# Attention and maxout network in one kernel: batch 2's row sums through one bank, broadcasts of batches 2 to 4 in the queue of the loads, and attention work in fewer, larger visits

## The chip, the cores and the metric

The kernel runs on one core of a Trainium2 chip. Its engines work side by side, each on its own list of instructions in order: TensorE (PE; its weight loads are shown apart as PEld), VectorE (DVE), ScalarE (ACT), GpSimd (POOL) and SyncE (SP). DMA engines move data, and DMAs are issued by POOL (in the profile's queue q0) and by SP (queue q1). Matrix products go to eight banks of PSUM memory, which DVE and ACT empty. The metric is the device time of one execution in microseconds (us): 407.24 us before the change, the median of three runs between 407.20 and 407.46.

## The reference, cut to what matters

There are 8 batches of 8 heads with 1024 positions of 64 numbers. Keys and values are first projected from 1024 positions down to 64, then every query attends to these 64, and the result goes through a network that takes the maximum of three products.

```python
k_proj = np.einsum('ks,bhsd->bhkd', E, k)
v_proj = np.einsum('ks,bhsd->bhkd', F, v)
scores = scale * np.matmul(q, k_proj.transpose(0, 1, 3, 2))
scores = scores - np.max(scores, axis=-1, keepdims=True)
attn = np.exp(scores)
attn = attn / (np.sum(attn, axis=-1, keepdims=True) + 1e-09)
attn_out = np.matmul(attn, v_proj)
x = attn_out.transpose(0, 2, 1, 3).reshape(B * S, H * D)      # 8192 x 512
h = np.maximum(np.maximum(x @ w1, x @ w2), x @ w3)            # 8192 x 768
out = h @ w_out                                               # 8192 x 512
```

## The kernel before, in words

The order of every engine is written out by hand. Batches follow one another, and each batch b is two chunks (`ch` 0 and 1) of 512 rows of the network. A chunk has six up steps (`up`, one for each 128 columns of h: 12 matmuls at L567, then a copy on ACT at L625 and two maxima on DVE at L629 and L577), and four down steps (`down`: six matmuls at L664, a copy of the result to `o_sb`, and after every second one an output store from SP). So PE's list is this network work, and between the steps stand visits of attention work for the *next* batch n = b + 1. The function `plan(b)` says which. Its key (ch, step) is the place: steps 0 to 5 are the up steps, 6 to 9 the down steps, and the work listed stands behind that step.

The pieces of attention work are these. `ld(b)` has POOL issue the loads of q, k and v of a batch (L200), each 1 MB as it lands; the tiles of k and v exist once, so k and v of a batch can only be issued after the projections of the batch before, and q only after the transposition of the q before it. `qd` copies q into another order on DVE and has SP issue a DMA transposition (L392). `kproj` and `vproj` project k and v (L345, 16 small matmuls each), `kt` turns the projected keys. A batch has four pairs of heads. `sc(n, g)` is one pair's score product (L211, four matmuls of 64x64 that run side by side, into two banks), followed by an exponential on ACT (L222) that frees these banks. With `now` the exponential is put into ACT's list at once; without it, behind the next `o_sb` copy or `h1s` copy (`run_later`). `za` takes a pair's row sums (four matmuls with ones, L231), their reciprocals on ACT (logarithm L291 and exponential L297), the value product (L231) and the multiplication on DVE (L308). `zc` and `vx` do the same work in another way: `zc` takes the sums of all four pairs into one bank (L256), their reciprocals (L262, L265), writes these 32 KB to the scratch tile `zd` in device memory (L268), and spreads them to all partitions with four broadcast DMAs of 512 KB into `zi_all` (L275), all issued by SP; `vx` is then the value product and the multiplication alone.

Banks are dealt when the program is built: `bank()` and `two()` take what a rough clock of the planner says comes free first. The real wait is a semaphore: a matmul that writes a bank waits for whoever read it last.

Before the change, batch 1 and batch 2 use `za`; batches 3 to 7 use `zc` and `vx`. Batch 2's four pairs are spread over five visits in batch 1's turn, batch 3's scores over two visits of two pairs, batch 4's scores stand one in batch 2's turn and three in batch 3's, and later batches' scores stand together in one visit with a value product between them.

Of the kernel before, what the change touches and what calls it, by code (L numbers as in the profile page):

```python
# [15 lines left out]
def kernel(  # L16
# [13 lines left out]
    nc = tc.nc  # L30
# [12 lines left out]
    NPAIR = H // 2  # L43
# [93 lines left out]
    def load_tiles(b):  # L137
        qkv[b] = tuple(
            loads.tile([P, H, SI, D], BF16, name=nm, bufs=n)
            for nm, n in (("q_t", 2), ("k_t", 1), ("v_t", 1))  # L140
        )
        return qkv[b]
# [51 lines left out]
    load_w(2, slice(2, 4))  # L194
    nc.gpsimd.dma_start(out=wout_sb, in_=moe_w_out.rearrange("(jt p) m -> p jt m", p=P))

    def load(b):
        tiles = load_tiles(b)
        for i in range(3):
            dma = nc.gpsimd.dma_start(out=tiles[i], in_=view((q, k, v)[i], b))  # L200
            if i == 0 and b - 1 in last_T:
                after(dma, last_T[b - 1])
# [42 lines left out]
            zi_alls[b] = att.tile([P, NPAIR, 2, CHUNK], FP32, name="zi_all", bufs=1)  # L245
        return zi_alls[b]

    def zc(b):

        def f():
            t, ns = bank()
            for hp in range(2):
                for g in range(NPAIR):
                    nc.tensor.matmul(  # L256
                        out=t[32 * g:32 * (g + 1), :], lhsT=pick[:, hp, :],
                        rhs=pTs[b, g, 0][:, hp, :], start=(hp == 0), stop=(hp == 1),
                    )
            ready = pe(2 * MM + 0.1)  # L260
            zlc = att.tile([P, CHUNK], FP32, name="zlc", bufs=1)
            nc.scalar.activation(out=zlc, in_=t, func=AF.Ln)  # L262
            runs("s", ready, 0.6, ns)
            zic = att.tile([P, CHUNK], FP32, name="zic", bufs=1)
            nc.scalar.activation(out=zic, in_=zlc, func=AF.Exp, scale=-1.0)  # L265
            when = runs("s", ready, 0.63) + 9.0
            zd = scratch.tile([NPAIR, 2, 2, CHUNK], FP32, name="zd")
            nc.sync.dma_start(  # L268
                out=zd.rearrange("g h c f -> (g h c) f"),
                in_=zic.rearrange("(a r) f -> a r f", r=8)[:, 0, :],  # L270
            )
            for u in range(2):
                gs = slice(2 * u, 2 * u + 2)
                for hp in range(2):
                    nc.sync.dma_start(  # L275
                        out=zi_all(b)[hp * HALF:(hp + 1) * HALF, gs],
                        in_=zd[gs, hp].partition_broadcast(HALF),
                    )
            for g in range(NPAIR):
                zis[b, g, 0] = zi_all(b)[:, g], when  # L280
        return f
# [98 lines left out]
    def qd(b, parts=1):  # L380

        def f():
            q_p = att.tile([P, NPAIR, SI, 2, D], BF16, name="q_p", bufs=1)
            qTs[b] = att.tile([P, NPAIR * SI, P], BF16, name="qT")
            n = NPAIR // parts
            for lo in range(0, NPAIR, n):
                for g in range(lo, lo + n):
                    copy(
                        "v", q_p[:, g].rearrange("p si h d -> p h si d"),
                        qkv[b][0][:, 2 * g:2 * g + 2], (), 0.43,  # L390
                    )
                last_T[b] = nc.sync.dma_start_transpose(  # L392
                    out=qTs[b][:, lo * SI:(lo + n) * SI, :],
                    in_=q_p[:, lo:lo + n].rearrange("p g si h d -> p (g si h d)"),
                )
        return f

    kps = {}
    def kproj(b):
        def f():  # L400
            t, ns = bank()
            proj(b, 1, t, (LO, HI), 4 * D)
            kps[b] = att.tile([P, 2, 2 * D], BF16, name="kp")
            copy("v", kps[b].rearrange("a g x -> a (g x)"), t[:, 0:4 * D], ns, 0.43)
        return f
# [18 lines left out]
    def vproj(b):  # L424
        def f():
            t, ns = bank()
            proj(b, 2, t, (LO, HI), 4 * D)

            vps[b] = att.tile([P, H, D], BF16, name="vp")
            for hh, hs in enumerate((LO, HI)):  # L430
                i = t[hh * HALF:(hh + 1) * HALF, 0:4 * D].rearrange("a (h d) -> a h d", d=D)
                for to in range(2):
                    copy("sv"[hh], vps[b][to * HALF:(to + 1) * HALF, hs, :], i, ns, 0.4)
        return f
# [244 lines left out]

    def ld(b):
        return lambda: load(b)

    def plan(b):
        n = b + 1
        if b == 0:
            c1 = (SPC, SPC)
            return {
                (0, 6): [za(0, 1, *c1), sc(0, 3, *c1)],  # L690
                (0, 7): [qd(1, 2), za(0, 2, *c1)],
                (0, 8): [za(0, 3, *c1)],
                (1, 0): [kproj(1)],
                (1, 1): [kt(1)],
                (1, 2): [vproj(1), ld(2)],
                (1, (3, "mid")): [sc(1, 0), sc(1, 1)],
                (1, 4): [za(1, 0), sc(1, 2)],
                (1, 5): [za(1, 1), sc(1, 3)],
                (1, 7): [za(1, 2), za(1, 3)],
            }  # L700
        if b == 1:
            return {
                (0, 1): [qd(2)],
                (0, 5): [kproj(2), vproj(2), ld(3)],
                (0, 6): [kt(2)],
                (0, 7): [sc(2, 0)],
                (0, 9): [za(2, 0), sc(2, 1)],
                (1, 1): [za(2, 1), sc(2, 2)],
                (1, 3): [za(2, 2), sc(2, 3)],
                (1, 5): [za(2, 3)],  # L710
                (1, 6): [qd(3)],
            }
        if b == 2:
            return {
                (0, 0): [kproj(3), vproj(3), ld(4)],
                (0, 1): [kt(3)],
                (0, 2): [sc(3, 0, now=True), sc(3, 1)],
                (0, 4): [sc(3, 2, now=True), sc(3, 3)],
                (0, 6): [zc(3)],
                (0, 7): [qd(4)],  # L720
                (1, 3): [kproj(4), vproj(4), ld(5), vx(3, 0), vx(3, 1)],
                (1, 4): [kt(4)],
                (1, 6): [vx(3, 2), vx(3, 3), sc(4, 0)],
            }
        if n == B:
            return {}
        out = {(0, 3): [zc(n)]}
        if n == 4:
            out[0, 1] = [sc(n, 1, now=True), sc(n, 2, now=True), sc(n, 3)]
        if n + 1 == B:  # L730
            out[1, 6] = [vx(n, g) for g in range(NPAIR)]
            return out
        out[0, 4] = [qd(n + 1)]
        out[1, 2] = [kproj(n + 1), vproj(n + 1), vx(n, 0), vx(n, 1), vx(n, 2)]
        out[1, 3] = [kt(n + 1)]
        out[1, 6] = [sc(n + 1, 0, now=True), vx(n, 3)]
        out[1, 6] += [sc(n + 1, g, now=True) for g in (1, 2)] + [sc(n + 1, 3)]
        if n + 2 < B:
            out[1, 3] += [ld(n + 2)]
        return out  # L740
# [61 lines left out]
```

## Time and profile before

| what | value |
|---|---|
| median of three runs | 407.24 us |
| the profiled execution | 407.2 us, of which its span is 405.4 us |
| granted PE clock in it | 1.00 |
| PE busy | 392.9 us (97%) |
| DVE, ACT, POOL busy | 203.3, 155.8, 31.4 us |
| matmuls of the network, L567 and L664 | 258.1 and 86.8 us busy |
| score products L211, value and sum products L231 (64x512) | 12.4 and 11.6 us busy |
| projections L345 of k and v | 7.5 and 7.3 us busy |
| queue q0 (POOL): packets, MB | 28512, 28.31 |
| queue q1 (SP): packets, MB | 37024, 35.16 |

An engine's row in order of time gives the start, how long a group of equal instructions took, the line, the operation, output and inputs, and in brackets how long the engine had sat idle before it and what released it. Matmuls overlap, so a group's length reaches a little into the next one; what counts is the distance from start to start. A DMA has an issue (a short instruction of POOL or SP) and a landing; the profile gives the time between the two.

### The profile page before, as it was taken

The numbers are of one execution on the slowest core, as the hardware profiler recorded it, in microseconds if no ns is written. First come the engines' busy times: TensorE is split into PE (matmuls) and PEld (weight loads), VectorE is DVE, ScalarE is ACT, GpSimd is POOL, SyncE is SP. The second block draws the span as 40 slices with busy tenths as digits, with TensorE's granted clock in tenths as the row PEclk, the third lists the DMA queues.
The fourth block names the chain that finished last, engine by engine and source line by source line (L and its number), as shares of the span: only waits on it lengthen the run. The fifth ranks groups of instructions, "written<-read, shape, count | busy, mean of one in ns | idle before, by whom it ended". The sixth has DMA issues, their size and how long they took to land.

```text
span 405.4 us, 5809 instructions
## 1 busy us (share of the span) xinstructions
PE 392.9 (97%) x2311; PEld 177.8 (44%) x2311; DVE 203.3 (50%) x319; ACT 155.8 (38%) x244; POOL 31.4 (8%) x44
## 2 busy tenths in 40 slices
PE   6999999999999999999999999999999999999996
PEld 3544443444445445444443444444443444444443
DVE  2348755762764535644472535725276342555251
ACT  2622447525673542353225332263314433132322
POOL 7330010001001100200020000100000000000000
PEclk9999999999999999999999999999999999999999
DMA  9999999959908999899999579990980229020202
GB/s 158 204 206 207 230 191 179 234 107 185 227 4 209 170 180 237 183 236 186 218 218 204 148 163 255 166 244 10 219 197 3 103 53 254 8 105 0 103 2 103
DMA packets 65707, 63.98 MB, mean 158 GB/s; under 512 B 30528, under 2 KB 58688, under 8 KB 65680
## 3 DMA queue, kind: packets, MB, share of 16 engines
q0 software_dynamic: 28512, 28.31, 44.0%
q1 hardware_dynamic: 37024, 35.16, 33.8%
q8 instruction: 18, 0.29, 0.3%
q10 hardware_dynamic: 144, 0.13, 0.1%
q14 instruction: 9, 0.07, 0.1%
HBM read 67.63 MB, written 16.94 MB: 209 GB/s over the span
## 4 chain that ended last, share of the span: by engine, by line
PE 80%; DMA 9%; DVE 5%; ACT 3%; issue 2%; SPq 0%; DVEq 0%; ACTq 0%
PE banks L567 52%; PE banks L664 18%; DMA v_t<-in_v_dram 7%; DVE xT L308 3%; PE banks L345 3%; PE banks L231 2%; PE banks L211 1%; DMA ef_f<-in_F_dram 1%; ACT pT L222 1%; ACT zl L291 1%; PE banks L441 1%; PE banks L256 1%; DVE m L629 1%; DVE vp L102 1%; DVE hT L577 1%
## 5 line engine op out<-in xcount | busy, mean ns | idle before, releaser
L567 PE MATMUL banks<-xT,w_sb 128*128 128x512 bf16 x1152 | 258.1, 379 | 0.9 <-DVE xT L308 0.6
L567 PEld LDWEIGHTS <-w_sb 128*128 128x128 bf16 x1152 | 110.0, 98 | 138.3 <-issue 9.7
L629 DVE TENSOR_TENSOR m<-banks,h1s 128x512 f32<-128x512 f32 x90 | 62.1, 690 | 130.6 <-ACT h1s L625 79.7
L625 ACT COPY h1s<-banks 128x512 f32<-128x512 f32 x90 | 52.6, 584 | 124.1 <-PE banks L567 122.0
L664 PE MATMUL banks<-wout_sb,hT 128*128 128x512 bf16 x378 | 86.8, 380 | 0.8 <-DVE xT L308 0.6
L577 DVE TENSOR_TENSOR hT<-banks,m 128x512 bf16<-128x512 f32 x90 | 62.3, 692 | 10.0 <-PE banks L567 0.8
L664 PEld LDWEIGHTS <-hT 128*128 128x128 bf16 x378 | 35.6, 98 | 47.2 <-DVE hT L577 4.1
L102 ACT COPY o_sb<-banks 128x512 f32<-128x512 f32 (+1 forms) x56 | 32.6, 582 | 55.2 <-PE banks L664 54.8
L308 DVE TENSOR_TENSOR xT<-banks,zi_all 128x1024 bf16<-128x1024 f32 x28 | 33.3, 1221 | 22.8 <-ACT zi_all L297 17.6
L222 ACT ACTIVATE pT<-banks 128x1024 bf16<-128x1024 f32 (+1 forms) x36 | 32.4, 932 | 18.8 <-PE banks L211 18.8
L200 POOL DMA_DIRECT2D q_t<-in_q_dram x7 | 6.2, 879 | 211.8 <-DMA qT<-q_p 104.7
L291 ACT ACTIVATE zl<-banks 128x512 f32<-128x512 f32 (+1 forms) x16 | 13.0, 810 | 9.8 <-PE banks L231 9.0
L211 PE MATMUL banks<-qT,kpT 64*64 64x512 bf16 (+1 forms) x144 | 12.4, 364 | 1.5 <-ACT pT L222 1.5
L345 PEld LDWEIGHTS <-efT 128*64 128x64 bf16 x224 | 11.6, 110 | 3.6 <-issue 3.0
L231 PE MATMUL banks<-pT,vp 64*64 64x512 bf16 (+1 forms) x144 | 11.6, 360 | 1.2 <-ACT zl L291 0.8
L102 DVE CAST vp<-banks 64x256 bf16<-64x256 f32 (+1 forms) x18 | 7.1, 397 | 11.1 <-ACT vp L102 4.3
L102 ACT CAST vp<-banks 64x256 bf16<-64x256 f32 x14 | 5.1, 364 | 19.2 <-PE banks L345 19.1
L102 DVE COPY q_p<-q_t 128x1024 bf16<-128x1024 bf16 x28 | 10.0, 419 | 0.0
L297 ACT ACTIVATE zi_all<-zl 128x1024 f32<-128x1024 f32 x8 | 8.5, 1057 | 0.3
L211 PEld LDWEIGHTS <-kpT 64*64 64x64 bf16 x144 | 4.2, 105 | 8.6 <-issue 6.3
L102 DVE COPY o_sb<-banks 128x512 f32<-128x512 f32 (+1 forms) x9 | 5.7, 653 | 4.5 <-PE banks L644 4.5
L345 PE MATMUL banks<-k_t,efT 128*64 128x256 bf16 x112 | 7.5, 276 | 0.0
(59 smaller groups left out, 121.1 us busy)
## 6 DMA issues: line engine op xcount, KB each, us to landing
out_dram<-o_sb SPq DMA_DIRECT2D x30, 512.0 KB, 4.0
zi_all<-zd SPq DMA_DIRECT2D x20, 512.0 KB, 7.9
q_t<-in_q_dram POOLq DMA_DIRECT2D x7, 1024.0 KB, 9.6
k_t<-in_k_dram POOLq DMA_DIRECT2D x7, 1024.0 KB, 14.4
v_t<-in_v_dram POOLq DMA_DIRECT2D x7, 1024.0 KB, 20.7
w_sb<-in_moe_w_dram POOLq DMA_DIRECT2D x5, 384.0 KB, 11.7
k_t<-in_k_dram POOLq DMA_DIRECT2D x2, 512.0 KB, 8.6
v_t<-in_v_dram POOLq DMA_DIRECT2D x4, 256.0 KB, 11.8
```

Source lines behind the costliest of these rows:

```text
L102: done = {"v": nc.vector.tensor_copy, "s": nc.scalar.copy, "g": nc.gpsimd.tensor_copy}[eng](out=o, in_=i)
L211: nc.tensor.matmul(out=t[c * HALF:(c + 1) * HALF, hp, 0:n * P], lhsT=kpTs[b][rows, g, :], rhs=qTs[b][rows, at:at + n, :], start=True, stop ...
L222: nc.scalar.activation(out=pTs[b, g, lo], in_=t, func=AF.Exp, scale=scale)
L231: nc.tensor.matmul(out=t[hp * HALF:(hp + 1) * HALF, c, 0:nsi * HALF], lhsT=w(rows, hp), rhs=p[rows, hp, :], start=True, stop=True,)
L291: nc.scalar.activation(out=zl, in_=t, func=AF.Ln)
L308: nc.vector.tensor_tensor(out=xTs[b][:, g, lo:lo + nsi, :].rearrange("a (c s) p -> a c (s p)", c=2), in0=t, in1=zi, op=ALU.mult,)
L345: nc.tensor.matmul(out=t[hh * HALF:(hh + 1) * HALF, 0:width], lhsT=efT[:, si, (kv - 1) * KP:kv * KP], rhs=qkv[b][kv][:, heads[hh], si, :], ...
L567: nc.tensor.matmul(out=h, lhsT=w_sb[i][:, ct, jt * P:(jt + 1) * P], rhs=xTs[b][:, ct, ch * SPC:(ch + 1) * SPC, :], start=(ct == first), st ...
L577: nc.vector.tensor_tensor(out=o, in0=h, in1=other, op=ALU.max)
L625: nc.scalar.copy(out=h1s, in_=h[0][0])
L629: nc.vector.tensor_tensor(out=m12, in0=h[1][0], in1=h1s, op=ALU.max)
L664: nc.tensor.matmul(out=o_ps, lhsT=hTs[b, ch][:, jt, tt * P:(tt + 1) * P], rhs=wout_sb[:, jt, :], start=(jt == 0), stop=(jt == NJT - 1),)
```

## The change

Batch 2 changes from `za` to `zc` and `vx`. `zc` gets a parameter for the engine that issues the four broadcasts: POOL for batches 2, 3 and 4, SP as before for 5 to 7. (The write of `zd` stays with SP.) `load` can issue some of a batch's three tiles: v of batches 4 and 5 is now issued on its own, behind the broadcasts of batch 3 and batch 4. The visits in the turns of batches 1, 2 and 3 are rearranged: all four score products of batches 2, 3 and 4 stand in one visit each; the projections of batch 3 move from behind up step 0 to behind up step 3; the value projection of batch 4 moves from batch 2's turn into batch 3's; batch 3's four value products stand in one visit behind the key projection of batch 4. Batch 0's turn and those from batch 4 on are as before.

```diff
-    def load(b):
-        tiles = load_tiles(b)
-        for i in range(3):
+    def load(b, which):
+        tiles = qkv[b] if b in qkv else load_tiles(b)
+        for i in which:
...
-    def zc(b):
+    def zc(b, queue=nc.sync):
...
-                    nc.sync.dma_start(
+                    queue.dma_start(
                         out=zi_all(b)[hp * HALF:(hp + 1) * HALF, gs],
                         in_=zd[gs, hp].partition_broadcast(HALF),
                     )
...
+        def scs(n):
+            return [sc(n, g, now=(g < NPAIR - 1)) for g in range(NPAIR)]
+
+        def vxs(n, gs):
+            return [vx(n, g) for g in gs]
+
         if b == 1:
             return {
-                (0, 1): [qd(2)],
-                (0, 5): [kproj(2), vproj(2), ld(3)],
-                (0, 6): [kt(2)],
-                (0, 7): [sc(2, 0)],
-                (0, 9): [za(2, 0), sc(2, 1)],
-                (1, 1): [za(2, 1), sc(2, 2)],
-                (1, 3): [za(2, 2), sc(2, 3)],
-                (1, 5): [za(2, 3)],
-                (1, 6): [qd(3)],
+                (0, 0): [qd(2)],
+                (0, 3): [kproj(2), vproj(2)],
+                (0, 4): [kt(2)],
+                (0, 5): scs(2),
+                (0, 7): [zc(2, nc.gpsimd), ld(3)],
+                (1, 3): vxs(2, (0, 1)),
+                (1, 6): vxs(2, (2, 3)),
+                (1, 7): [qd(3)],
             }
         if b == 2:
             return {
-                (0, 0): [kproj(3), vproj(3), ld(4)],
-                (0, 1): [kt(3)],
-                (0, 2): [sc(3, 0, now=True), sc(3, 1)],
-                (0, 4): [sc(3, 2, now=True), sc(3, 3)],
-                (0, 6): [zc(3)],
-                (0, 7): [qd(4)],
-                (1, 3): [kproj(4), vproj(4), ld(5), vx(3, 0), vx(3, 1)],
-                (1, 4): [kt(4)],
-                (1, 6): [vx(3, 2), vx(3, 3), sc(4, 0)],
+                (0, 3): [kproj(3), vproj(3), ld(4, (0, 1))],
+                (0, 4): [kt(3)],
+                (0, 6): scs(3),
+                (0, 8): [zc(3, nc.gpsimd), ld(4, (2,))],
+                (0, 9): [qd(4)],
+                (1, 6): [kproj(4)] + vxs(3, range(NPAIR)),
+                (1, 7): [kt(4), ld(5, (0, 1))],
             }
...
         out = {(0, 3): [zc(n)]}
         if n == 4:
-            out[0, 1] = [sc(n, 1, now=True), sc(n, 2, now=True), sc(n, 3)]
+            out[0, 1] = scs(n)
+            out[0, 3] = [zc(n, nc.gpsimd), vproj(n), ld(n + 1, (2,))]
...
         out[0, 4] = [qd(n + 1)]
-        out[1, 2] = [kproj(n + 1), vproj(n + 1), vx(n, 0), vx(n, 1), vx(n, 2)]
+        out[1, 2] = [kproj(n + 1), vproj(n + 1)] + vxs(n, (0, 1, 2))
```

More of the change, by code (lines that the diff above doesn't have):

```diff
@@ L678, in down, with ld @@
             nc.sync.dma_start(out=ov[:, si - 1:si + 1, :], in_=o_sb)
-    def ld(b):
-        return lambda: load(b)
+    def ld(b, which=(0, 1, 2)):
+        return lambda: load(b, which)
     def plan(b):
@@ L728, in plan @@
         if n == 4:
-            out[0, 1] = [sc(n, 1, now=True), sc(n, 2, now=True), sc(n, 3)]
+            out[0, 1] = scs(n)
+            out[0, 3] = [zc(n, nc.gpsimd), vproj(n), ld(n + 1, (2,))]
         if n + 1 == B:
-            out[1, 6] = [vx(n, g) for g in range(NPAIR)]
+            out[1, 6] = vxs(n, range(NPAIR))
             return out
         out[0, 4] = [qd(n + 1)]
-        out[1, 2] = [kproj(n + 1), vproj(n + 1), vx(n, 0), vx(n, 1), vx(n, 2)]
+        out[1, 2] = [kproj(n + 1), vproj(n + 1)] + vxs(n, (0, 1, 2))
         out[1, 3] = [kt(n + 1)]
-        out[1, 6] = [sc(n + 1, 0, now=True), vx(n, 3)]
-        out[1, 6] += [sc(n + 1, g, now=True) for g in (1, 2)] + [sc(n + 1, 3)]
+        out[1, 6] = scs(n + 1)
+        out[1, 6][1:1] = vxs(n, (3,))
         if n + 2 < B:
```

## The prediction

> **What bounds the kernel now.** I read the page first, then the tensor engine's own order of time, then the waits in it, then the DMA issues with their landings. The page:
>
> ```profile
> span 405.4 us, 5809 instructions
> PE 392.9 (97%) x2311; PEld 177.8 (44%) x2311; DVE 203.3 (50%) x319; ACT 155.8 (38%) x244; POOL 31.4 (8%) x44
> PE 80%; DMA 9%; DVE 5%; ACT 3%; issue 2%; SPq 0%; DVEq 0%; ACTq 0%
> ```
>
> TensorE (PE) is the bound, at a granted clock of 1.00 throughout. The twelve microseconds in which it idles lie at the start, at the end and in small waits around visits of attention work. So the change is worth what it does to PE's order, plus every microsecond in which PE has to wait for a late transfer. Three kinds of wait already in the trace say what the new order will cost. First, one visit in which four score products (L211) and one value product (L231) stand together, in batch 3's second chunk:
>
> ```profile
> 214.58 0.41 PE L211 MATMUL banks<-qT,kpT 64*64 64x512 bf16 x4
> 215.04 0.70 PE L211 MATMUL banks<-qT,kpT 64*64 64x512 bf16 x8
> 216.25 0.41 PE L211 MATMUL banks<-qT,kpT 64*64 64x512 bf16 x4 [0.52 <-ACT pT L222]
> ```
>
> Each score product takes two of the eight banks. The fifth user of banks waits until the exponential of the first has ended. What ScalarE (ACT) does meanwhile:
>
> ```profile
> 215.17 2.86 ACT L222 ACTIVATE pT<-banks 128x1024 bf16<-128x1024 f32 x3
> 218.10 0.58 ACT L102 COPY o_sb<-banks 128x512 f32<-128x512 f32 x1
> 218.58 1.03 ACT L222 ACTIVATE pT<-banks 128x1024 bf16<-128x1024 f32 x1
> ```
>
> The reader should see that the fourth exponential ends at 219.61, which is 5.0 us after the visit began. Second, four value products together (batch 7's, near the end):
>
> ```profile
> 354.84 1.15 PE L231 MATMUL banks<-pT,vp 64*64 64x512 bf16 x16
> 356.58 4.05 PE L664 MATMUL banks<-wout_sb,hT 128*128 128x512 bf16 x18 [0.59 <-DVE xT L308]
> ```
>
> They take 1.74 us from start to the next work, where 16 matmuls at 54 ns and an exit of 0.13 would take 0.99: a wait of 0.75 for VectorE (DVE) to empty the first pair of banks. Third, the transfers. Loads are issued by GpSimd (POOL):
>
> ```profile
> 23.47 0.87 POOL L200 DMA_DIRECT2D k_t<-in_k_dram  x1 [0.31 <-PE banks L496]
> 25.34 0.87 POOL L200 DMA_DIRECT2D v_t<-in_v_dram  x1 [1.00 <-PE banks L567]
> ...
> 130.37 0.89 POOL L200 DMA_DIRECT2D q_t<-in_q_dram  x1 [37.07 <-DVE hT L577]
> 131.24 0.88 POOL L200 DMA_DIRECT2D k_t<-in_k_dram  x1
> 132.11 0.89 POOL L200 DMA_DIRECT2D v_t<-in_v_dram  x1
> ```
>
> and the issues view, asked for single issues (last column: us to landing), has, in this order, the three loads at 130 to 132, the first and last of four broadcasts of the reciprocals (issued by SP at 149.2 and 151.2), a transposition alone (82.0), and the k and v loads of 23.5 and 25.3:
>
> ```profile
> q_t<-in_q_dram POOLq DMA_DIRECT2D x1, 1024.0 KB, 9.6
> k_t<-in_k_dram POOLq DMA_DIRECT2D x1, 1024.0 KB, 13.8
> v_t<-in_v_dram POOLq DMA_DIRECT2D x1, 1024.0 KB, 18.1
> ...
> zi_all<-zd SPq DMA_DIRECT2D x1, 512.0 KB, 4.9
> ...
> zi_all<-zd SPq DMA_DIRECT2D x1, 512.0 KB, 10.4
> ...
> qT<-q_p SPq DMA_TRANSPOSE x1, 6.7
> ...
> k_t<-in_k_dram POOLq DMA_DIRECT2D x1, 1024.0 KB, 23.6
> v_t<-in_v_dram POOLq DMA_DIRECT2D x1, 1024.0 KB, 30.2
> ```
>
> Adding issue and landing: loads land at 140.0, 145.0, 150.2, one after another, 5.1 us each. Broadcasts land at 154.1 and 161.6, 2.5 us each. The last pair lands at 47.1 and 55.5: the v load took 8.4 instead of 5.1, because an output store and two half transpositions (L392) ran beside it. In before, batch 3's loads land by 112.6 and batch 5's by 190.8, each more than 10 us ahead of use. That cover is what the change spends.
>
> **The change part by part.** Times of the changed order count from batch 1's first up product (74.55, unchanged), with 0.216 per 128x512 matmul: 2.59 per up step, 1.295 per down step, 1.87 for both projections, a visit's entry 0.09 and exit 0.13.
>
> Removed from PE. (a) Batch 2's sums: four groups of four matmuls against ones, 0.24 each (104.32 to 104.56), become one group against the picking matrix, 0.55 (182.79 to 183.34): -0.40. (b) Three visits fewer in batches 1 and 2 (12 become 9), 0.22 each: -0.66. (c) Waits that go: PE's 0.38 for the lone exponential at 97.2 and 0.26 for banks at 166.5: -0.64. Sum -1.7. ACT also loses four pairs of 1.02 + 1.06 and DVE nothing; both are half idle, so no gain from that.
>
> Added to PE, by the rows above. (d) Batches 2, 3, 4 now have four score products in one visit. All eight banks are then taken, and the next down or up step uses the first pair. It starts 1.55 us after the visit's start (0.47 to ACT, 1.03, 0.05), or 1.67 where an o_sb copy stands ahead on ACT, against 0.99 without a wait: 0.56 + 0.68 + 0.56 = +1.8. (e) The one-bank sums of batches 2 and 3 now stand only two down steps behind these scores. PE is there 1.55 + 2.59 + 0.09 = 4.2 us (4.35 in batch 2's turn) after the visit's start, the fourth exponential ends at 4.9 to 5.05: 0.7 each, +1.4. Batch 4's stand two up steps behind, 6.7 us, and wait for nothing. (f) Four value products of batch 3 in one visit, behind a projection whose copy DVE makes first: 0.75 + 0.16 = +0.9. Net of (a) to (f): **+2.4 us**. Bounds: +1 if the waits of (e) are half, +3.2 if (c) does not go.
>
> Queues. zd stays on SP; the four broadcasts of batches 2, 3 and 4 go to POOL behind the zd wait, and ahead of the next load, which can no longer be issued before they are. SP's transpositions are freed (12 us of issue behind broadcasts, 4.8 without), but only a q load waits for them, so that gains nothing.
>
> (g) Batch 3's v. Sums of batch 2 at 96.5, ended 97.8 with (e). zd issued 1.4 later (231.49 to 232.90), landed 1.8 later (same store), POOL wakes 0.55 later (88.7 to 89.25): 101.5. First broadcast from POOL: no row. Between 4.9 (SP's) and 9.6 (a first load); a load's 9.6 less its 5.1 plus 2.4 gives 6.9, I take 6.7. Then 3 x 2.4 and three loads at 5.1: v lands at 130.8. PE asks for it at 122.4 + 10.4 + 1.0 = 133.8. Undisturbed, 3.0 early. But an output store at 120.6 costs 1.4 (two of them delay the loads at 206.7 by 2.8, a landing of 20.9 against 18.1), and batch 3's transposition is issued at 122.3. Of the 8.4 above, about 2 in 5.6 us are lost to transpositions: a load beside one runs at 0.65. The 7.6 us left take 11.8, and v lands at 136.3: PE waits **2.5 us** (0 to 4).
>
> (h) Batch 5's v is the worst. From the start t of batch 4's sums PE needs 0.55 + 0.94 + 5.18 + 5.18 + 7.77 + 0.1 + 0.94 = 20.7 us until it asks for this v. The transfer comes at 0.55 + 1.4 + 1.8 + 0.55 + 6.7 + 7.2 + 5.1 = 23.3. Late by 2.7 undisturbed (0.9 with SP's 4.9). Batch 5's transposition, 1 MB, is issued at about t + 6.4 and runs beside all of it. At 0.65 for the load, 2.7 more; for the broadcasts no row, between 0.65 and 1, I take 0.85: 1.7 more. PE waits **7.1 us** (1 to 12, the latter with 0.65 for all and the stores).
>
> At no cost: batch 2's q copies one up step earlier (1.42 us of DVE, which then has over 1 us of idle time before each pair of maxima until 90). The first half of batch 2's broadcasts lands at 110.6 for a multiplication (L308) due on DVE at 111.2; the maxima queue behind it, and PE would only miss a bank if it came 3 us later. Batch 3's q (120.4) is copied at 120.8. Batch 4's k and v and batch 5's q and k have over 7 us left.
>
> Sum against this execution's time: 405.4 of span, 407.2 reported, the median being 407.24. +2.4 + 2.5 + 7.1 = +12.0: **419 us**.
>
> Two rules of the Trainium skill weigh on this. "DMA: Bandwidth & Descriptors" (Anatomy of one DMA - SWDGE) fits a transfer from GpSimd with 2.0 us plus bytes over 436 GB/s. The trace's 2.4 to 2.5 us per 512 KB and 5.1 per load are twice its variable part; by the rule (h) would land well before it is asked for, (g) too, and the sum would be an estimated 409.6. The other speaks against the change: "TensorE: Matmul & The Clock Gate" (Part 1) says that an idle window of some 3.4 us halves the clock for about as long. The longest idle time in this trace is 1.87 us (to 7.70), with the clock at 1.00 after it, so no run here shows it; by the rule a wait as in (h) would cost an estimated 1.7 us on top, 421.
>
> **Rivals.**
> A. The v loads are in time: broadcasts from POOL start as fast as SP's and the transposition yields. For it: undisturbed, (h) is short by only 0.9 to 2.7. Then 407.2 + 2.4 = 409.6, to 412 with a remnant. Against: the 8.4 us load.
> B. Faster: PE's new waits don't form, the banks and exponentials being free when PE comes. Place: (d), (e), (f). Price: 4.1 of wait gone leaves -1.7, 405.5. It decides only from the point where these waits sum to under 1.7 us and the loads are in time as in A. Against: the waits of 0.52 and 0.75 in the trace.
> C. The transposition takes more of the engines than I assume: (g) 4, (h) 12: 425.6.
>
> **How the numbers follow.** Forecast (413 to 423) 0.46, C (over 423) 0.15, A (408.1 to 413) 0.28, B and what else ends faster 0.08, within 0.2% 0.03. Told from no change: about 0.8 us either way. The range 409 to 426 takes in A's centre and C's. Slower 0.89, same 0.03, faster 0.08.
>
> **What the changed profile would show.** Right: PE's waits at L345 before batch 3's and batch 5's v product, released by the v load's DMA, about 2 and 7 us; 0.5 to 0.7 after each four-score visit, released by L222, and in L256 for batches 2 and 3; POOL's broadcasts landing 2.4 us apart; SP's transpositions slower than 6.7. Wrong: no PE idle time over 1 us at L345 (A), or none at L256 (B); or a broadcast that lands much faster from POOL.

## The result and the profile after

The changed kernel takes **412.98 us** (median of four executions, 412.77 to 414.75) against 407.35 for the kernel before on the same chip (four executions, 407.20 to 408.96). The ratio is 1.0139, 95% interval [1.0101, 1.0177]. In a second comparison it took 412.74 (five executions) against 407.83 (eleven), a ratio of 1.0122 [1.0104, 1.014]. It is slower by 5.6 and 4.9 us, where the forecast was 11.8 over the median. The direction and the range held; the size is a little under half of what was forecast. The ratios leave out one execution of 426.66 us at a granted clock of 0.983, of the filled kernel's second comparison below, which took far longer than the other five of that kernel.

The page of the changed kernel, and below it, in a second fence, the waits of PE (in all, times, longest, in us):

```profile
span 413.0 us, 5793 instructions
PE 395.9 (96%) x2303; PEld 179.9 (44%) x2303; DVE 203.3 (49%) x319; ACT 148.8 (36%) x238; POOL 38.7 (9%) x56
PEclk9999999999999999999989999999999999999999
PE 83%; DMA 6%; ACT 4%; DVE 3%; issue 2%; POOL 0%; SPq 0%; DVEq 0%; ACTq 0%
```

```profile
PE banks L345 <- DMA v_t<-in_v_dram: 2.9, 1, 2.9
...
PE banks L664 <- DVE xT L308: 1.3, 2, 0.7
PE banks L664 <- ACT pT L222: 0.8, 2, 0.5
...
PE banks L256 <- ACT pT L222: 0.3, 2, 0.2
```

PE still sets the end. New are a wait for a v load, of one batch and not of two, and waits for exponentials (L222) at the down steps and the sums; the wait for VectorE (L308) at a down step now comes twice. The mark 8 in the row of the clock stands where PE came out of the wait for v.

The profiled execution (414.75) began 2.25 us late in work that the change does not touch, so it is compared turn by turn, beside a second profile of the changed kernel from the second comparison. A turn runs from its first up product to that of the next batch:

| turn of batch | before | changed | changed, second profile |
|---|---|---|---|
| 1 | 74.55 to 122.19: 47.64 | 76.80 to 124.46: 47.66 | 74.93 to 122.59: 47.66 |
| 2 | to 171.46: 49.27 | to 173.88: 49.42 | to 172.00: 49.41 |
| 3 | to 220.49: 49.03 | to 228.31: 54.43 | to 225.75: 53.75 |
| sum against before | | +5.57 | +4.88 |

Nearly all of the loss lies in batch 3's turn, where PE waits for v of batch 5. PE's rows there:

```profile
205.80 1.06 PE L345 MATMUL banks<-k_t,efT 128*64 128x256 bf16 x16
209.77 1.67 PE L345 MATMUL banks<-v_t,efT 128*64 128x256 bf16 x16 [2.91 <-DMA v_t<-in_v_dram]
211.37 1.49 PE L231 MATMUL banks<-pT,vp 64*64 64x512 bf16 x12
212.80 3.08 PE L567 MATMUL banks<-xT,w_sb 128*128 128x512 bf16 x12
215.72 0.28 PE L412 MATMUL banks<-ident,kp 128*128 128x128 bf16 x2
```

In the kernel before, the two products and the turning of the keys (L412):

```profile
201.60 1.06 PE L345 MATMUL banks<-k_t,efT 128*64 128x256 bf16 x16
202.50 1.04 PE L345 MATMUL banks<-v_t,efT 128*64 128x256 bf16 x16
...
207.66 0.27 PE L412 MATMUL banks<-ident,kp 128*128 128x128 bf16 x2
```

From the key product to L412 it is 9.92 us in the changed kernel and 6.06 in the kernel before. The changed kernel's stretch in windows of 2 us (busy time of PE, PEld, DVE, ACT and POOL, then the granted clock, the DMA share and GB/s):

```profile
209.00:211.00 2.00, 1.23 (x14) 1.09 (x16) 0.00 (x0) 0.00 (x0) 0.00 (x0) 0.77 1.07 220
211.00:213.00 2.00, 2.00 (x19) 0.50 (x14) 0.73 (x2) 0.73 (x2) 0.48 (x1) 0.50 1.16 392
213.00:215.00 2.00, 2.00 (x9) 0.84 (x8) 1.97 (x3) 0.58 (x1) 2.00 (x3) 0.88 0.71 249
```

After the idle time the clock is at 0.50: the v product takes 1.60 us from start to start instead of 0.97 in the kernel before, and the value products 1.43 instead of 0.78. The next up step makes up part of it (2.92 instead of 3.41): the wait of 0.21 for VectorE that the kernel before has in this step is gone.

The transfer that comes late, in the rows of POOL and in the issues (the last column is us to landing, first of the four broadcasts alone, then v and the transposition beside it):

```profile
190.24 2.49 POOL L275 DMA_DIRECT2D zi_all<-zd  x4 [20.56 <-DVE m L629]
192.72 0.91 POOL L200 DMA_DIRECT2D v_t<-in_v_dram  x1
```

```profile
zi_all<-zd POOLq DMA_DIRECT2D x1, 512.0 KB, 4.9
...
v_t<-in_v_dram POOLq DMA_DIRECT2D x1, 1024.0 KB, 17.0
...
qT<-q_p SPq DMA_TRANSPOSE x1, 19.8
```

The broadcasts land at 195.2, 197.6, 200.0 and 202.3, v at 209.7. The transposition, 6.7 when alone, takes 19.8 here.

And the four-score visit of batch 3 with the sums behind it, which stand for the new waits of PE in general:

```profile
143.48 1.15 PE L211 MATMUL banks<-qT,kpT 64*64 64x512 bf16 x16
145.15 2.75 PE L664 MATMUL banks<-wout_sb,hT 128*128 128x512 bf16 x12 [0.52 <-ACT pT L222]
147.83 0.40 PE L256 MATMUL banks<-pT,pick 128*32 128x512 bf16 x3
148.39 0.59 PE L256 MATMUL banks<-pT,pick 128*32 128x512 bf16 x5 [0.16 <-ACT pT L222]
```

From start to start the visit takes 1.67 us and the sums 1.08, which is 0.68 and 0.53 more than without a wait (0.99 and 0.55): all eight banks are taken by the scores, and the fourth exponential is not done when the sums want it.

### The profile page after: what moved, and what is told of

It is laid out like the page before. It is cut to its first block, busy times and chain, and to the rows that moved or that the text cites. A ratio compares the mean times of both kernels' runs of the same rounds, so it can differ in the third digit from the quotient of the medians.

```text
span 413.0 us, 5793 instructions
## 1 busy us (share of the span) xinstructions
PE 395.9 (96%) x2303; PEld 179.9 (44%) x2303; DVE 203.3 (49%) x319; ACT 148.8 (36%) x238; POOL 38.7 (9%) x56
## 4 chain that ended last, share of the span: by engine, by line
PE 83%; DMA 6%; ACT 4%; DVE 3%; issue 2%; POOL 0%; SPq 0%; DVEq 0%; ACTq 0%
PE banks L567 56%; PE banks L664 17%; DMA v_t<-in_v_dram 4%; PE banks L345 3%; ACT pT L222 3%; DVE xT L308 3%; PE banks L231 2%; DMA ef_f<-in_F_dram 2%; PE banks L211 1%; ACT zl L291 1%; PE banks L441 1%; PE banks L256 1%; PE banks L356 1%; PE banks L470 0%; POOL zi_all L275 0%
## 5 line engine op out<-in xcount | busy, mean ns | idle before, releaser
L308 DVE TENSOR_TENSOR xT<-banks,zi_all 128x1024 bf16<-128x1024 f32 x28 | 33.1, 1220 | 12.0 <-PE banks L231 5.4
L222 ACT ACTIVATE pT<-banks 128x1024 bf16<-128x1024 f32 (+1 forms) x36 | 32.0, 936 | 18.5 <-PE banks L211 18.5
L102 DVE CAST vp<-banks 64x256 bf16<-64x256 f32 (+1 forms) x18 | 7.1, 397 | 15.8 <-ACT vp L102 8.4
L275 POOL DMA_DIRECT2D zi_all<-zd x12 | 7.3, 619 | 76.2 <-DMA zd<-zic 55.6
L211 PE MATMUL banks<-qT,kpT 64*64 64x512 bf16 (+1 forms) x144 | 12.0, 364 | 1.6 <-ACT pT L222 1.6
L291 ACT ACTIVATE zl<-banks 128x512 f32<-128x512 f32 (+1 forms) x12 | 8.9, 739 | 5.2 <-PE banks L231 4.4
L345 PE MATMUL banks<-v_t,efT 128*64 128x256 bf16 x112 | 8.0, 288 | 2.9 <-DMA v_t<-in_v_dram 2.9
L211 PEld LDWEIGHTS <-kpT 64*64 64x64 bf16 x144 | 4.5, 105 | 9.3 <-issue 6.8
L441 PE MATMUL banks<-warm_f 128*128 128x512 f32 x8 | 6.6, 970 | 1.5 <-DVE warm_f L175 1.5
## 6 DMA issues: line engine op xcount, KB each, us to landing
k_t<-in_k_dram POOLq DMA_DIRECT2D x7, 1024.0 KB, 15.2
```

Of the source, the lines that this page charges most:

```text
L102: done = {"v": nc.vector.tensor_copy, "s": nc.scalar.copy, "g": nc.gpsimd.tensor_copy}[eng](out=o, in_=i)
L211: nc.tensor.matmul(out=t[c * HALF:(c + 1) * HALF, hp, 0:n * P], lhsT=kpTs[b][rows, g, :], rhs=qTs[b][rows, at:at + n, :], start=True, stop ...
L222: nc.scalar.activation(out=pTs[b, g, lo], in_=t, func=AF.Exp, scale=scale)
L291: nc.scalar.activation(out=zl, in_=t, func=AF.Ln)
L308: nc.vector.tensor_tensor(out=xTs[b][:, g, lo:lo + nsi, :].rearrange("a (c s) p -> a c (s p)", c=2), in0=t, in1=zi, op=ALU.mult,)
L345: nc.tensor.matmul(out=t[hh * HALF:(hh + 1) * HALF, 0:width], lhsT=efT[:, si, (kv - 1) * KP:kv * KP], rhs=qkv[b][kv][:, heads[hh], si, :], ...
```

## The experiments

Two questions: what makes v late, and what is left when it is not? All kernels compute everything that the changed kernel does; the runs that fill the wait only add matmuls that nobody reads.

### Is the loss the wait for v? Two ways to take it away

**The load of v ahead of the broadcasts.** Batch 4's v projection, and with it the load of batch 5's v, stands one up step earlier than the broadcasts:

```diff
-            out[0, 3] = [zc(n, nc.gpsimd), vproj(n), ld(n + 1, (2,))]
+            out[0, 2] = [vproj(n), ld(n + 1, (2,))]
+            out[0, 3] = [zc(n, nc.gpsimd)]
```

> The changed kernel with one order turned: in batch 3's turn the value projection of batch 4 stands one up step earlier, and the load of batch 5's v directly behind it, so that POOL issues this load ahead of batch 4's four broadcasts. Theory 1 (the 3.0 us wait at 206.74 is the load's place behind the broadcasts, and the half clock after it is the wait's consequence): the load is issued near 185 and lands near 196 in that execution's time, 10 us before it is asked for; no wait, clock 1.00 from 210 to 215. The median falls by 3.0 of wait and by the 1.35 of slow matmuls (0.70 at the v product, 0.65 at the value products), less about 0.5 that the wait had given back to VectorE: 412.98 to about 409.1, so 1.7 to 1.8 above before. The broadcasts land near 202 and are asked for near 207. Rival (the 5.6 us come from the merged visits on PE and the wait was cover for them, e.g. VectorE being behind): falls by under 1 us. Rival (the load ahead delays the broadcasts past their use): the wait returns at the value products, released by L308.

Measured: 409.23 us (nine executions), ratio to before 1.0035 [1.0022, 1.0047].

**Batch 4's broadcasts on SP again**, so that v is issued without them in front:

```diff
-            out[0, 3] = [zc(n, nc.gpsimd), vproj(n), ld(n + 1, (2,))]
+            out[0, 3] = [zc(n), vproj(n), ld(n + 1, (2,))]
```

> The changed kernel with batch 4's four broadcasts issued by SP, as in the kernel before; batches 2 and 3 keep theirs on POOL. Batch 5's v is then issued by POOL as soon as the value projection of batch 4 is done (187.5 in that execution). Theory 1 (what makes v late is the order within POOL's queue, not the engines' total): load and broadcasts share the engines from 192 on, the load ends well before 206: no wait, about 409.1. Rival (the DMA engines have no room for 2 MB of broadcasts, 1 MB of load and the transposition in these 19 us): v lands after 206.7 in any case, and the time is over 411.

Measured: 409.26 us (seven executions), ratio 1.0035 [1.0021, 1.005]. In the first kernel v lands at 193.3 and is wanted at 205.6; in this one it lands at 202.2. PE's rows of the first:

```profile
204.69 1.06 PE L345 MATMUL banks<-k_t,efT 128*64 128x256 bf16 x16
205.58 1.04 PE L345 MATMUL banks<-v_t,efT 128*64 128x256 bf16 x16
210.75 0.27 PE L412 MATMUL banks<-ident,kp 128*128 128x128 bf16 x2
```

From the key product to L412 it is 6.06 us, as before the change. Both ways give the same time, 3.5 to 3.8 us below the changed kernel's two medians. The late v is shown to be most of the loss, and the order in POOL's queue is what makes it late. Some 1.4 us over the kernel before remain.

### Does the transposition beside it make v late?

**Batch 5's transposition after the last down step** of the first chunk, where the load should have been over:

```diff
-        out[0, 4] = [qd(n + 1)]
+        out[0, 9 if n == 4 else 4] = [qd(n + 1)]
```

> The changed kernel with batch 5's q copies and transposition five steps later (behind the last down step of batch 3's first chunk instead of behind up step 4), so that the transposition doesn't run beside batch 5's v load. Theory 1 (beside the transposition the v load streams at 0.69 of its rate, 7.4 instead of 5.1 us, and the broadcasts not slower): v lands 5.1 us after the last broadcast, the wait at the v product falls from 3.0 to 0.7, the clock stays at 1.00: about 409.6. Rival (the 7.4 us are the price of a load behind broadcasts in one queue, whatever runs beside): v lands 7.4 after the last broadcast, wait 3.0, time as the changed kernel's, 413.

Measured: 415.73 us, ratio 1.0199 [1.0172, 1.0225], a miss, and slower than the changed kernel. Its issues, in the stretch from 182 to 202 us:

```profile
v_t<-in_v_dram POOLq DMA_DIRECT2D x1, 1024.0 KB, 18.8
out_dram<-o_sb SPq DMA_DIRECT2D x2, 512.0 KB, 8.1
...
qT<-q_p SPq DMA_TRANSPOSE x1, 15.4
```

The transposition, issued at 197.6, still lay beside the whole load (200.6 to 209.9). And the output stores, which SP had held back behind the long transposition, now ran there too: the load took 9.3 us from the last broadcast's landing, not 7.4. The broadcasts were no faster without the transposition beside them: 2.3 to 2.4 us apart, as with it.

**The transposition in the second chunk, behind v's projection** (one execution):

```diff
-        out[0, 4] = [qd(n + 1)]
+        if n != 4:
+            out[0, 4] = [qd(n + 1)]
...
-        out[1, 3] = [kt(n + 1)]
+        out[1, 3] = [kt(n + 1)] + ([qd(n + 1)] if n == 4 else [])
```

> The changed kernel with batch 5's q copies and transposition behind the key turn in the second chunk, after the v product, so that no transposition is issued before batch 5's v has landed. (Five steps later had not been enough: the transposition was then issued at 197.6 and ran beside the whole load, which took 9.3 us after the last broadcast.) Theory 1 (a load beside a transposition is slowed, broadcasts are not): v lands 5.1 us after the last broadcast, up to 6.5 if an output store runs beside it, against 7.4 in the changed kernel and 9.3 with the later transposition; broadcasts 2.4 apart as ever; the wait at the v product falls from 3.0 to between 0.7 and 2.1. Batch 5's scores then wait some us for the transposition, so the time says nothing. Rival (a load behind broadcasts takes 7 to 9 us whatever else runs): v lands 7 us or more after the last broadcast.

Measured: 419.03 us. The load took 8.65 us behind the last broadcast with no transposition near it:

```profile
v_t<-in_v_dram POOLq DMA_DIRECT2D x1, 1024.0 KB, 18.2
out_dram<-o_sb SPq DMA_DIRECT2D x2, 512.0 KB, 8.2
```

In the transposition's place stood two stores of 512 KB, issued at 194.3 and 196.9 and landed at 202.8 and 204.7. Scores of batch 5 then had to wait 3.5 us for the transposition as well, on top of 4.0 us for v. That a load behind broadcasts takes 7 us whatever runs beside it is contradicted by batch 2's broadcasts in the changed kernel, with nothing beside the q load behind them: 116.0 to 121.2, 5.2 us. So it is 5.2 alone, 7.4 beside a transposition, 8.65 beside two stores, 9.3 beside both. The kernel before has a row beside two stores as well: the v load issued at 208.41 took 8.2 us behind the k load. How much of the 9.3 belongs to which is not told apart: moving the one moved the other, and no kernel here had this window free of both. So the question is answered in part: a transposition beside the load goes with 2.2 us more, but taking it away let the stores in, and v came no sooner.

### Does the halved clock cost time?

Thirteen matmuls that nobody reads fill the wait, so that PE is not idle in it:

```diff
-        out[1, 2] = [kproj(n + 1), vproj(n + 1)] + vxs(n, (0, 1, 2))
+        out[1, 2] = [kproj(n + 1)] + ([lambda: idle(13)] if n == 4 else [])
+        out[1, 2] += [vproj(n + 1)] + vxs(n, (0, 1, 2))
```

> The changed kernel with 13 idle matmuls of 128x512 (2.8 us, result unused) on PE between batch 5's key projection and its value projection, where PE waits 3.0 us. Nothing else is moved. Theory 1 (the wait costs its 3.0 us, and the half clock seen from 209 to 213.5 costs about 0.85 more, net of what VectorE catches up): the clock stays at 1.00 there, the v product takes 0.94 instead of 1.64, the value products 0.77 instead of 1.43, and the time falls by 0.8 to 1.3, to about 411.9. Rival (the clock share in the record costs nothing on the way, or the added matmuls just take its place): 413, or more by up to 0.3.

Measured: 412.62 us (six executions, 411.82 to 415.21), ratio 1.0106 [1.0087, 1.0125]. Expected was about 411.9. The stretch from the key product to L412 took 9.31 us at a clock of 1.00, against 9.92. But this was not beside the changed kernel on one chip, so both ran again together:

> The changed kernel, unaltered, beside the next run on the same chip. Both theories: 412.8 to 413.0, with the wait of about 2.9 us before batch 5's v product. It is there to be compared with the run that fills that wait.

> The changed kernel with 13 matmuls of 128x512 that nobody reads, between batch 5's k and v products, so that the wait for v is filled with 2.8 us of TensorE work; v itself lands as late as before. Theory (the wait costs its own 2.9 us and then 0.6 to 0.9 us through the halved clock): 0.6 to 0.9 below the changed kernel on the same chip. Rival (the halved clock is made up for by VectorE's catching up, and costs nothing): within 0.2 of it.

Measured: the changed kernel 412.74 (five executions), the filled one 412.79 (six, or 412.65 without the one of 426.66), ratios 1.0122 [1.0104, 1.014] and 1.0125 [1.0107, 1.0143]: no difference that can be told. The second profile of the changed kernel says why the first had misled. PE's rows and the windows of the same stretch:

```profile
203.92 1.06 PE L345 MATMUL banks<-k_t,efT 128*64 128x256 bf16 x16
207.98 1.06 PE L345 MATMUL banks<-v_t,efT 128*64 128x256 bf16 x16 [3.00 <-DMA v_t<-in_v_dram]
208.97 0.84 PE L231 MATMUL banks<-pT,vp 64*64 64x512 bf16 x12
209.75 2.07 PE L567 MATMUL banks<-xT,w_sb 128*128 128x512 bf16 x8
...
213.17 0.27 PE L412 MATMUL banks<-ident,kp 128*128 128x128 bf16 x2
```

```profile
209.00:211.00 2.00, 2.00 (x19) 0.66 (x18) 1.10 (x3) 0.91 (x3) 0.26 (x1) 1.00 1.19 383
```

Here an idle time of 3.00 us left the clock at 1.00, and the stretch took 9.25. So the halving comes in some executions and not in others. Where it comes it cost this stretch 9.92 - 2.91 against 9.25 - 3.00, 0.76 us. Of the second comparison's five executions of the changed kernel two had a mean clock of 1.00 (spans 410.4 and 410.6) and three of 0.994 to 0.996 (411.0, 411.1, 412.2). These means don't say where the clock fell: the first profile of the changed kernel (mean 0.992) has one halved stretch behind this wait and another from 8.68 to 12.10, and the filled kernel's first profile (also 0.992) has its halved stretch from 7.95 to 14.78 and none here. The theory that the halving costs the median 0.6 to 0.9 gets no support; with intervals of some 0.7 us to either side, these runs don't exclude it.

Where the idle time lies seems to decide. In the first profile the two halved stretches, from 8.68 and from 210.07, each last 3.41 us and begin 59 such steps apart. Counted in these steps, the 2.91 us of idle time lay within one of them (206.66 to 210.07). In the second profile, counted from the first change of the clock in its trace (5.27), the 3.00 us lay across two, 1.67 us in the one and 1.33 in the other. Idle times of 4.04 and 4.61 us, in the two runs above that move the transposition, go with 3.41 and 6.83 us at 0.50, one step and two; 8.54 us, in the next run below, with 10.24, three steps. No run moved the idle time alone, so this is read from traces and not tested.

### What is left without the wait for v: PE's own waits

**The one-bank sums one down step later**, on top of the v load ahead (first experiment), so that the exponentials are done:

```diff
-                (0, 7): [zc(2, nc.gpsimd), ld(3)],
+                (0, 8): [zc(2, nc.gpsimd), ld(3)],
...
-                (0, 8): [zc(3, nc.gpsimd), ld(4, (2,))],
-                (0, 9): [qd(4)],
+                (0, 9): [zc(3, nc.gpsimd), ld(4, (2,)), qd(4)],
```

> The kernel with batch 5's v load ahead of the broadcasts (409.2), and the one-bank sums of batches 2 and 3 one down step later, three down steps behind their scores instead of two. Theory 1 (the sums, 1.08 us from start to next work instead of 0.55, wait 0.53 each for the fourth exponential): L256 takes 0.55 in both batches, the time falls by 1.07, to 1.8 - 1.07 = 0.8 above before, about 408.2. Rival (that wait only covers another one, e.g. of the following down step for a bank or of batch 3's multiplications for broadcasts that now land 0.8 later): falls by under 0.4.

Measured: 417.84 us, ratio 1.0249 [1.0234, 1.0263], a miss by the mechanism of its rival. The sums lost their 0.53 each (0.55 from start to start). But batch 3's broadcasts came late. The four broadcasts and batch 4's transposition in the issues, and PE's rows behind them:

```profile
zi_all<-zd POOLq DMA_DIRECT2D x4, 512.0 KB, 18.2
...
qT<-q_p SPq DMA_TRANSPOSE x1, 29.1
```

```profile
165.13 1.06 PE L231 MATMUL banks<-pT,vp 64*64 64x512 bf16 x16
174.73 2.72 PE L664 MATMUL banks<-wout_sb,hT 128*128 128x512 bf16 x6 [8.54 <-DVE xT L308]
```

The transposition was now issued 0.6 us behind the write of `zd` (1.2 in the changed kernel), with batch 4's k load still running. That load landed 9.7 us behind the q load (6.8 in the changed kernel), `zd` took 6.2 (3.6), and the first broadcast landed 15.2 us after its issue (9.7). From the issue of `zd` to the last broadcast's landing it was 30.1 us instead of 21.7, and PE stood behind the value products for 8.5 us until VectorE had multiplied by what they bring. That the transposition's place is the cause is argued from this order; two output stores moved with it.

**Visits parted two and two**, again with v ahead: scores of batches 2, 3 and 4 in two visits of two, batch 3's value products likewise, and batch 2's projections one up step earlier so that the sums keep their place. The core of it:

```diff
+        def two_of(n, gs):
+            return [sc(n, g, now=True) for g in gs]
...
-                (0, 5): scs(2),
+                (0, 4): two_of(2, (0, 1)),
+                (0, 5): two_of(2, (2, 3)),
...
-                (0, 6): scs(3),
+                (0, 5): two_of(3, (0, 1)),
+                (0, 6): two_of(3, (2, 3)),
...
-                (1, 6): [kproj(4)] + vxs(3, range(NPAIR)),
-                (1, 7): [kt(4), ld(5, (0, 1))],
+                (1, 6): [kproj(4)] + vxs(3, (0, 1)),
+                (1, 7): vxs(3, (2, 3)) + [kt(4), ld(5, (0, 1))],
```

> The kernel with batch 5's v load ahead of the broadcasts, and the merged visits taken apart again: the scores of batches 2, 3 and 4 in two visits of two pairs each behind neighbouring steps (batch 2's projections one step earlier for it), batch 3's four value products two and two. Sums in one bank, and broadcasts of batches 2 to 4 on POOL, stay. Theory 1 (of the 1.8 us that PE's order still loses, the waits in the merged visits are 0.55 + 0.68 + 0.55 behind the scores, 1.07 in the sums and 0.75 behind four value products, 3.6 together, against four more visits at 0.22): 1.8 - 3.6 + 0.9 = 0.9 below before, about 406.5. Rival (merging visits gains what it was meant to, the losses lie elsewhere in the order): no faster than 409.2, or slower by the four visits' 0.9.

Measured: 407.46 us (eleven executions), ratio 1.0004 [0.9985, 1.0022]: as before the change, where 0.9 below it was expected. PE's rows where batch 2's scores and sums stand:

```profile
90.33 0.63 PE L211 MATMUL banks<-qT,kpT 64*64 64x512 bf16 x8
90.89 2.76 PE L567 MATMUL banks<-xT,w_sb 128*128 128x512 bf16 x12
93.58 0.63 PE L211 MATMUL banks<-qT,kpT 64*64 64x512 bf16 x8
...
96.84 0.61 PE L256 MATMUL banks<-pT,pick 128*32 128x512 bf16 x8
```

No wait is left in them: 0.56 for each visit and 0.55 for the sums. From the first up product of batch 1 to batch 5's sums it is 156.00 us, against 158.26 with v ahead alone and 156.39 before the change. So the waits for full banks and for the fourth exponential were the other part of the loss. What the change saves on PE is 0.39 by this trace and nothing that the times can tell.

**The later batches parted as well** in that kernel, their scores two and two and their value products two and two, from batch 3's turn on. The kernel before has the same full visits there:

```diff
-            out[1, 6] = vxs(n, range(NPAIR))
+            out[1, 4], out[1, 6] = vxs(n, (0, 1)), vxs(n, (2, 3))
...
-        out[1, 2] = [kproj(n + 1), vproj(n + 1)] + vxs(n, (0, 1, 2))
+        out[1, 2] = [kproj(n + 1), vproj(n + 1)] + vxs(n, (0, 1))
...
-        out[1, 6] = scs(n + 1)
-        out[1, 6][1:1] = vxs(n, (3,))
+        out[1, 4] = vxs(n, (2, 3))
+        out[1, 5], out[1, 7] = two_of(n + 1, (0, 1)), two_of(n + 1, (2, 3))
```

> The same, and the later batches' visits, which the change left as they were, taken apart likewise: two of the value products move two steps on, scores two and two behind the last up step and the second down step, batch 7's four value products two and two. From the trace of before: in each of three turns 0.83 behind three value products and 0.78 in the visit with four scores, 0.24 twice at that visit's entry, 0.75 in batch 7's: 6.1 of waits against seven more visits at 0.22, so 4.5 below the previous kernel, about 402 and 5.4 below before. Rival (PE would wait elsewhere, ACT being behind at the down steps): 404 or more.

Measured: 403.18 us (six executions), ratio 0.9902 [0.9886, 0.9918], faster than both kernels. The gain over the kernel before is 4.4 us, where 5.4 was expected. The same edit to the later batches **in the kernel before**, with nothing of the change:

```diff
-            out[1, 6] = [vx(n, g) for g in range(NPAIR)]
+            out[1, 4], out[1, 6] = [vx(n, 0), vx(n, 1)], [vx(n, 2), vx(n, 3)]
...
-        out[1, 2] = [kproj(n + 1), vproj(n + 1), vx(n, 0), vx(n, 1), vx(n, 2)]
+        out[1, 2] = [kproj(n + 1), vproj(n + 1), vx(n, 0), vx(n, 1)]
...
-        out[1, 6] = [sc(n + 1, 0, now=True), vx(n, 3)]
-        out[1, 6] += [sc(n + 1, g, now=True) for g in (1, 2)] + [sc(n + 1, 3)]
+        out[1, 4] = [vx(n, 2), vx(n, 3)]
+        out[1, 5] = [sc(n + 1, g, now=True) for g in (0, 1)]
+        out[1, 7] = [sc(n + 1, g, now=True) for g in (2, 3)]
```

> The kernel before, with the four-score visits of the later batches (from batch 4's turn on) parted two and two and the value products parted likewise; nothing else of the change. If parting these visits is what made the fully split kernel beat the kernel before by 4.4 us (403.2), and the change's own rearrangement of batches 1 to 3 is worth only the 0.4 us that its split form showed, this kernel ends at about 403.2 to 403.6. Rival: the parting of the later visits needs the rearranged front (batch 4's broadcasts and batch 5's v earlier); then it ends above 405.

Measured: 403.37 us (six executions), ratio 0.9898 [0.988, 0.9915]. The two ratios agree, so the gain is that of the parting, and the change's front adds nothing to it that can be told. In this kernel's batch 3 turn, where the kernel before had three value products together, and all four scores with the fourth value product in one visit:

```profile
203.70 0.63 PE L231 MATMUL banks<-pT,vp 64*64 64x512 bf16 x8
204.26 2.76 PE L567 MATMUL banks<-xT,w_sb 128*128 128x512 bf16 x12
...
209.66 0.63 PE L231 MATMUL banks<-pT,vp 64*64 64x512 bf16 x8
210.22 2.76 PE L567 MATMUL banks<-xT,w_sb 128*128 128x512 bf16 x12
212.91 0.63 PE L211 MATMUL banks<-qT,kpT 64*64 64x512 bf16 x8
213.47 2.76 PE L664 MATMUL banks<-wout_sb,hT 128*128 128x512 bf16 x12
```

No row has a bracket: there are more visits and no waits. The turns of batches 3 to 6 are shorter by 1.40, 1.16, 1.40 and 0.22 us, 4.2 together.

## Why the prediction had the direction right and the size wrong

**(a) to (f), work and waits on PE: right, 0.5 us too large.** Predicted +2.4. The second profile's turns give 4.88 - 3.00 = 1.9. The four-score visits (d) took 1.54, 1.67 and 1.54 where 1.55, 1.67 and 1.55 stood. The sums (e) waited 0.53 each, not 0.7: the first three of their eight matmuls don't need the fourth exponential and ran ahead of it. The four value products (f) took 1.74, a wait of 0.75; the 0.16 added for the copy ahead of them did not come. These two make up the 0.5. The savings (a) to (c) were not measured singly; with the other terms as measured, their -1.7 fits the sum.

**(g), batch 3's v: failed.** Predicted to land 2.5 us late, it landed at 133.9, 1.9 before it was asked for at 135.8, so PE did not wait. POOL's issue at 103.59 stood within 0.2 us of where it was put (101.5, and 2.25 for the late start). The issues, v's landing, and PE's v product:

```profile
103.59 2.38 POOL L275 DMA_DIRECT2D zi_all<-zd  x4 [40.43 <-DMA zd<-zic]
...
107.69 0.95 POOL L200 DMA_DIRECT2D v_t<-in_v_dram  x1
```

```profile
v_t<-in_v_dram POOLq DMA_DIRECT2D x1, 1024.0 KB, 26.2
```

```profile
135.81 1.04 PE L345 MATMUL banks<-v_t,efT 128*64 128x256 bf16 x16
```

The first broadcast landed 5.3 us after its issue (6.7 assumed). Three more took 2.36 each, as assumed. q took 5.2 and k 5.0, and v 7.7 beside a store and a transposition: contention cost 2.6 us where 5.6 were set (1.4 for the store, 4.2 for the transposition). That is the term that failed. The v load's rate beside its neighbours, 5.1 / 7.7 = 0.66, is about the 0.65 assumed; but the prediction put this rate on 7.6 us of loading, where only v's 5.1 us ran so slowly, and added 1.4 for the store, beside which the k load took 5.0. The rest of the margin came from the first broadcast, which was 1.4 us sooner.

**(h), batch 5's v: the mechanism right, the size more than twice too large.** Predicted 7.1, measured 2.9 and 3.0. From the start of batch 4's sums, at 185.96:

| step | predicted | measured |
|---|---|---|
| sums, reciprocals, `zd` landed, POOL awake | 4.3 | 4.3 |
| first broadcast | 6.7 | 4.95 |
| three more | 7.2 | 7.1 |
| slowing of the broadcasts by the transposition | 1.7 | 0 |
| v behind them, slowing included | 7.8 | 7.4 |
| landed | 27.7 | 23.8 |
| asked for | 20.7 | 20.8 |

Two terms failed. The first broadcast was 1.75 us too long: it had no row from POOL, and 6.7 was formed from a load's 9.6; from POOL it took 4.95, as from SP (4.9). The row of the same operation on the other queue was the nearer one. And the 1.7 for broadcasts beside a transposition is nothing: they landed 2.3 to 2.4 us apart, and the transposition took 19.8. The prediction found no row for this, but the kernel before has one: SP's four broadcasts for batch 4 land there at 194.3, 196.7, 199.1 and 201.4, with a transposition issued behind them in the same queue at 192.0 that takes 14.1. The load beside it did run at 5.1 / 7.4 = 0.69, near the 0.65 assumed. Of the other rows v's load was 0.4 too long, and the rest held to 0.1 us.

**The rivals.** The medians (412.98 and 412.74) lie at the upper edge of the bracket that the prediction gave to A (408.1 to 413), not in the forecast's. A's conditions were met in part: POOL's broadcasts were as fast as SP's, the transposition left them alone, and batch 3's v was in time; but the transposition did go with a slower load, batch 5's v was late, and A's remnant is this 3.0. B, that the new waits on PE do not form, is refuted by the rows of L211 and L256. C is refuted: the transposition took less, not more.

**The two rules of the skill.** The broadcasts landed 2.3 to 2.4 us apart. What "DMA: Bandwidth & Descriptors" (Anatomy of one DMA - SWDGE) gives for the variable part of 512 KB at its 436 GB/s is an estimated 1.2, so the trace's rows decide here, and the sum by the rule, an estimated 409.6, leaves out a wait that does form. For the loads the prediction's comparison counted the 1 MB that lands; the kernel reads 2 MB of f32 for it, for which the rule's variable part is an estimated 4.8, near the 5.0 to 5.2 of undisturbed loads. The clock was 0.50 behind 2.91 us of idle time in one execution and stayed at 1.00 behind 3.00 in another. "TensorE: Matmul & The Clock Gate" (Part 1) speaks of a window of some 3.4 us; the halved stretches of 3.41 us agree with it, and the 0.76 us that the halving cost in the one execution are under the estimated 1.7.

## What to carry to other kernels

Before work is put in front of a load in a queue, add up the load's lead over its use from rows of the same kind of transfer, taking the nearest operation even when it ran on another queue: here the lead was over ten microseconds and the new order spent it and three more. A transfer's price depends on its neighbours, and delaying one neighbour lets the next one in. Score and value products that fill all banks at once cost 0.5 to 0.8 us of waits a visit on this TensorE-bound kernel; two pairs a visit, with a network step between, waited for nothing and won 1% in the kernel before.

## What the runs showed of the hardware that was not expected

- A transposition issued behind POOL's broadcasts leaves them as they are and takes long itself; one issued ahead goes with a late first broadcast. In the changed kernel's batch 4, issued 2.2 us behind the first broadcast, it left this at 4.95 us and the others 2.3 to 2.4 apart, and took 19.8 itself instead of 6.7. In batch 3, issued 3.0 us ahead of the first broadcast, it landed after 15.8, and that broadcast took 9.7; with v's load first and the transposition issued 1.7 us ahead, the first broadcast took 9.9.
- A load of 1 MB behind other transfers took longer beside two output stores (8.65 us in one execution, 8.2 in the kernel before) than beside a transposition (7.4 to 7.5 in three profiles).
- The same idle time of about 3 us halved the clock for 3.41 us in one execution, where it lay within one step of 3.41 us, and not in another, where it lay across two.
